# A fused retention and gated feed-forward kernel: the hand-written list of its first two groups is reordered, with other queues for the first loads

## The chip, the cores and the metric

The kernel runs on one core of a Trainium2 chip. The time is the time on the device in microseconds (us) of one execution. Three runs of the kernel before gave 237.85, 241.09 and 242.36 us. A profile of one execution, with every instruction and every transfer, lies beside them; its times are us from its first instruction.

The engines are TensorE (PE; PEld are its weight loads), VectorE (DVE), ScalarE (ACT), GpSimd (POOL) and SyncE (SP). SP and GpSimd issue transfers, each in the order of its own instructions; the 16 DMA engines carry them out.

## What is computed

Per batch and head a decayed state is kept, and the result goes through a normalised SwiGLU layer. Cut to what matters:

```python
for t in range(S):                       # B, H, S, D = 4, 8, 768, 64
    state = gamma * state + einsum('bhd,bhe->bhde', k[:, :, t], v[:, :, t])
    y[:, :, t] = scale * einsum('bhd,bhde->bhe', q[:, :, t], state)
x = y.transpose(0, 2, 1, 3).reshape(B * S, H * D)        # 3072 x 512
xn = x / sqrt(mean(x * x) + 1e-6) * rms_g
g = xn @ w_gate                          # 512 x 1536
out = (g * sigmoid(g) * (xn @ w_val)) @ w_out            # 1536 x 512
```

## The kernel before, in words

The sequence is cut into 6 chunks of 128 positions; a unit of the attention part is one chunk of one batch (c, b). A group of the feed-forward part is one chunk of all four batches, 512 rows. Products are in bfloat16 with 128x128 weights and up to 512 columns.

The order of all work is written by hand in the string ORDER (lines 17 to 99). Each word is one step; the loop at lines 487 to 491 reads it and calls a function of that name. A word is `name.chunk.batch@engine/banks`: @S, @P, @D, @A are SP, GpSimd, DVE and ACT, and the digits behind / are the PSUM banks. Every engine runs its own steps in the order in which the words stand; waits between engines come from the data, the buffers and the banks.

The steps of one unit:

- Lq, Lk, Lv (line 262) load 128 rows of q, k, v, 256 KB of float32 in DRAM. On SP they land as float32, and Cq, Ck (lines 285, 287, 293) turn them into bfloat16. On GpSimd q and k are turned into bfloat16 on the way; v stays float32.
- V (line 303, or eight small steps on ACT, line 301) multiplies v by a decay, vdec, into vp.
- Tq, Tk (line 309) transpose q and k on TensorE, Eq, Ek (line 142) copy the result out of PSUM. In chunks 2 to 5 tq, tk do both by a DMA transpose on SP (line 319).
- A (line 335) makes the scores, M0 and M1 (line 343) multiply them by a mask on DVE: in chunk 0 the decay mask mask0, else the 0/1 mask causal.
- Y (lines 353 and 357) multiplies them by vp and, from chunk 1 on, adds q times the state. In chunks over 0, x (line 364) multiplies by the decay ydec.
- S (line 371, ACT) sums the squares, R (lines 377 and 379, GpSimd) makes the reciprocal root, N (line 385, DVE) scales by it and by g_bc, which is rms_g on every partition. X (line 398) transposes xn on TensorE, XE (lines 142 and 404) copies it to xnT, or does both by a DMA transpose when it is @S.
- K (line 413) makes the chunk's contribution to the state, U (lines 142 and 421) adds it, B (line 428, GpSimd) copies the state to bfloat16 for the next chunk.

The feed-forward steps: g and v (line 436) multiply column blocks n0 to n1 of w_gate and w_val with the rows of batches b0 to b1 of a chunk; s (line 446, ACT) is the SiLU, h (line 454, DVE) the product of both, d (line 461) the product with w_out, over blocks n0 to n1, o and st copy and store it. `g.0.2.3.0.3` is block 2 for batches 0 to 2 of chunk 0. wg, wv and wo (lines 271 and 278) load column pieces of the three weights through GpSimd, turned into bfloat16: 256 columns (wg.0.2, wg.2.4, wg.4.6), 384 columns (wg.6.9, wg.9.12), and 512 rows of w_out (wo.0.4, wo.4.8, wo.8.12). hot.n (line 216) issues n products that nothing uses, fillers for TensorE.

Constants: iota (line 220) is the select that prepares row_f, from which mk0 and mk1 (line 243, ACT, four steps each) make mask0; ident and causal are further selects on GpSimd; vd and yd (lines 234 and 238, ACT) make vdec and ydec; tab (line 250) makes ACT load the table of the SiLU early; rms (line 254) loads rms_g to all 128 partitions as g_bc.

In the kernel before, q, k, v of unit (0, 0) and g_bc come through SP, all else of chunks 0 and 1 and all weights through GpSimd's queue. Its list starts so:

```python
ident Lq.0.0@S hot.48/0 Lq.0.1@P Lk.0.0@S Lk.0.1@P vd yd iota Lv.0.0@S Lv.0.1@P Lk.0.2@P mk0 Lq.0.2@P Cq.0.0@D
Ck.0.0@A Lv.0.2@P Tk.0.0/0 Tq.0.0/1 mk1 wg.0.2 hot.8/3 Ek.0.0@D Eq.0.0@D Tq.0.1/2 wv.0.2 V.0.0@D A.0.0/34
```

Loads of chunk 2 wait for the last piece of w_out (line 264). From chunk 2 on, q, k and v all come through SP.

Of the kernel before, what the change touches and what calls it, by code (L numbers as in the profile page):

```python
# [22 lines left out]
s.0.0.2.0.1 X.0.1/1 S.0.2 v.0.0.2.0.1/2 XE.0.1@D R.0.2 g.0.0.2.1.2/4 K.0.0/0 v.0.0.2.1.2/5 s.0.0.2.1.2 N.0.2
U.0.0@A hot.3/1 h.0.0.2.0.1 X.0.2/3 B.0.0 Tq.0.3/7 V.0.3@A XE.0.2@D hot.4/0 v.0.0.2.2.3/1 wg.4.6 v.0.2.3.0.3/4
Eq.0.3@D Lq.1.0@P g.0.0.2.2.3/6 h.0.0.2.1.2 Tk.0.3/0 v.0.3.4.0.3/2 Lk.1.0@P Ek.0.3@A g.0.3.4.0.3/3 Lq.1.1@P
s.0.0.2.2.3 A.0.3/75 s.0.3.4.0.3 g.0.2.3.0.3/0 M1.0.3 Lk.1.2@P M0.0.3 v.0.4.5.0.3/6 s.0.2.3.0.3 wg.6.9 Y.0.3/3
g.0.5.6.0.3/5 Lv.1.0@P causal S.0.3 h.0.2.3.0.3 v.0.5.6.0.3/7 R.0.3 h.0.3.4.0.3 Tk.1.0/0 h.0.0.2.2.3
g.0.4.5.0.3/4 N.0.3 Ek.1.0@A Tq.1.0/2 wv.9.12 s.0.4.5.0.3 X.0.3/1 Eq.1.0@D K.0.2/0 s.0.5.6.0.3 K.0.1/3 XE.0.3@D
A.1.0/42 g.0.4.6.3.4/5 wv.6.9 M0.1.0 g.0.0.4.3.4/1 U.0.2@A U.0.1@A h.0.5.6.0.3 v.0.4.6.3.4/4 M1.1.0
g.0.8.9.0.4/0 s.0.4.6.3.4 h.0.4.5.0.3 v.0.0.4.3.4/3 s.0.0.4.3.4 Lk.1.1@P g.0.7.8.0.4/7 wg.9.12 V.1.0@D Tk.1.2/2  # L30
g.0.6.7.0.4/5 B.0.2 s.0.8.9.0.4 h.0.4.6.3.4 B.0.1 Y.1.0/6 v.0.11.12.0.4/1 Ek.1.2@A Lq.1.2@P h.0.0.4.3.4 K.1.0/0
wo.0.4 v.0.6.7.0.4/4 x.1.0 v.0.7.8.0.4/2 S.1.0 Tq.1.1/3 v.0.8.9.0.4/6 s.0.6.7.0.4 Eq.1.1@D R.1.0 g.0.11.12.0.4/3
h.0.8.9.0.4 Lq.1.3@P U.1.0@D Tk.1.1/5 s.0.7.8.0.4 g.0.9.10.0.4/6 N.1.0 Lv.1.1@P g.0.10.11.0.4/0 Ek.1.1@A
h.0.7.8.0.4 B.1.0 A.1.1/75 s.0.11.12.0.4 K.0.3/2 Lk.1.3@P d.0.0.0.4/3 h.0.11.12.0.4 U.0.3@A M0.1.1 wo.4.8
d.0.2.0.4/1 M1.1.1 Tq.1.3/2 d.0.3.0.4/7 h.0.6.7.0.4 Tq.1.2/5 Lv.1.2@P v.0.9.10.0.4/4 Eq.1.3@A V.1.1@D
s.0.10.11.0.4 Eq.1.2@D Lv.1.3@P Y.1.1/2 s.0.9.10.0.4 v.0.10.11.0.4/5 x.1.1 B.0.3 h.0.9.10.0.4 Tk.1.3/0 S.1.1
wo.8.12 X.1.0/6 d.0.1.0.4/2 h.0.10.11.0.4 Ek.1.3@A R.1.1 XE.1.0@D A.1.2/45 A.1.3/06 d.0.0.4.8 N.1.1 M1.1.2
d.0.1.4.8 V.1.2@P M0.1.3 d.0.3.4.8 M0.1.2 V.1.3@P M1.1.3 K.1.2/5 Y.1.2/0 U.1.2@D X.1.1/4 Y.1.3/6 x.1.2 XE.1.1@A
B.1.2 K.1.3/5 d.0.2.4.8 x.1.3 S.1.2 U.1.3@D Lq.2.0@S S.1.3 d.0.0.8.12 R.1.2 Lk.2.0@S d.0.2.8.12 Lv.2.0@S R.1.3
N.1.2 o.0.0@A st.0.0@S d.0.1.8.12 B.1.3 N.1.3 o.0.2@A Lq.2.1@S X.1.2/4 X.1.3/0 o.0.1@A d.0.3.8.12 XE.1.2@D  # L40
Cq.2.0@P XE.1.3@A Lk.2.1@S K.1.1/6 g.1.3.4.0.4/5 o.0.3@A U.1.1@D Ck.2.0@P tq.2.0 v.1.1.2.0.4/3 B.1.1 s.1.3.4.0.4
g.1.0.1.0.4/1 st.0.3@S V.2.0@P st.0.2@S g.1.6.7.0.4/2 s.1.0.1.0.4 Lv.2.1@S tk.2.0 Cq.2.1@P g.1.1.2.0.4/4
# [60 lines left out]
def kernel(  # L103
# [152 lines left out]
    def load(n, e, c, b):
        if e is POOL and n != "v":
            x = ring([128, H, D], BF16, n + "b", {"q": 6, "k": 8}[n])
            t[c, b][n + "b"] = x
# [2 lines left out]
        i = done[n, c, b] = e.dma_start(out=x, in_=rows[n][b, c])  # L262
# [259 lines left out]
```

## Time and profile before

| what | value |
|---|---|
| runs | 237.85, 241.09, 242.36 us (median 241.09) |
| profiled execution: span from first to last instruction | 236.7 us (its own time is not listed apart) |
| needed product first on TensorE (transposed k of unit 0, 0) | 6.56 us |
| first feed-forward product | 15.85 us |
| first feed-forward product of chunk 1 | 61.18 us |
| TensorE busy in 0 to 5, 5 to 10, 10 to 15, 15 to 20 us | 3.89, 3.90, 4.43, 4.73 us |
| TensorE's granted clock | 1.000 |
| HBM read and written | 28.57 and 6.29 MB |

A line of the timeline gives the start, the time from the start of the first to the end of the last instruction of a row, the engine, the line of the kernel, the operation, output<-inputs, the shapes and the number of instructions; a bracket names idle time in front of it and what ended it. In the chain of waits a row is start, duration and what the end of the execution hung on then. A line of the DMA issues gives how many there were, the KB of each, and the median us from issue to landing. Busy time of TensorE includes fillers and the time that products take to drain.

### The profile page before, as it was taken

To read this page: it belongs to the slowest core of one execution; us is meant where nothing else is said; L and a number is where in the kernel's file an instruction comes from. 1 tells how busy PE (TensorE), PEld (TensorE's weight loads), DVE (VectorE), ACT (ScalarE), POOL (GpSimd) and SP (SyncE) were. 2 spreads that over 40 slices of the span, in tenths; PEclk is the share of its full clock that TensorE was granted. 3 is DMA by queue.
4 is the path that set the end of the run, shared out by engine and by line. 5 is a ranking of instruction groups with operands and counts; after the bars stand their busy time and mean duration, and the time that the engine had idled before them with its cause. 6 is when DMAs were issued, how large, how long until landed. Compare 5 with 4: busy or idle time off the path is not lost.

```text
span 236.7 us, 4515 instructions
## 1 busy us (share of the span) xinstructions
PE 227.5 (96%) x1729; PEld 123.5 (52%) x1729; DVE 121.1 (51%) x212; ACT 87.7 (37%) x187; POOL 109.5 (46%) x182
## 2 busy tenths in 40 slices
...
GB/s 142 206 208 160 149 206 188 126 209 130 235 231 210 191 195 154 194 248 123 39 233 171 179 204 158 198 138 141 215 216 74 0 25 95 38 47 0 44 44 134
DMA packets 105045, 34.89 MB, mean 147 GB/s; under 512 B 94464, under 2 KB 101504, under 8 KB 105024
## 3 DMA queue, kind: packets, MB, share of 16 engines
...
q10 hardware_dynamic: 144, 0.10, 0.1%
...
HBM read 28.57 MB, written 6.29 MB: 147 GB/s over the span
## 4 chain that ended last, share of the span: by engine, by line
PE 71%; DMA 13%; POOL 6%; DVE 3%; issue 2%; ACT 1%; SPq 1%; POOLq 0%; DVEq 0%; ACTq 0%
PE v_ps L436 22%; PE o_ps L461 21%; PE g_ps L436 21%; DMA vf<-in_v_dram 4%; DMA wo_b<-in_moe_w_out_dram 3%; DMA kb<-in_k_dram 3%; DMA wg_b<-in_moe_w_gate_dram 3%; PE y_ps L353 2%; PE y_ps L357 1%; PE a_ps L335 1%; POOL kb L262 1%; PE kv_ps L413 1%; PE o_ps L483 1%; DVE xn L385 1%; POOL vp L303 1%
## 5 line engine op out<-in xcount | busy, mean ns | idle before, releaser
L454 DVE TENSOR_TENSOR hT<-sg,v_ps 128x512 bf16<-128x512 bf16 (+2 forms) x75 | 48.7, 663 | 63.2 <-ACT sg L446 32.0
L436 PE MATMUL v_ps<-xnT,wv_b 128*128 128x512 bf16 (+2 forms) x328 | 70.9, 353 | 1.2 <-DVE am L343 1.1
L436 PE MATMUL g_ps<-xnT,wg_b 128*128 128x512 bf16 (+2 forms) x328 | 70.8, 353 | 0.4 <-DMA wg_b<-in_moe_w_gate_dram 0.3
L446 ACT ACTIVATE sg<-g_ps 128x512 bf16<-128x512 f32 (+2 forms) x75 | 43.3, 581 | 65.3 <-PE g_ps L436 56.3
L461 PE MATMUL o_ps<-wo_b,hT 128*128 128x512 bf16 x276 | 63.5, 379 | 0.9 <-DMA wo_b<-in_moe_w_out_dram 0.9
L436 PEld LDWEIGHTS <-wv_b 128*128 128x128 bf16 x328 | 29.4, 98 | 30.7 <-DMA xnT<-xn 1.5
L436 PEld LDWEIGHTS <-wg_b 128*128 128x128 bf16 x328 | 29.5, 98 | 29.7 <-DMA wg_b<-in_moe_w_gate_dram 0.5
L461 PEld LDWEIGHTS <-hT 128*128 128x128 bf16 x276 | 26.1, 98 | 29.5 <-issue 0.9
L142 ACT COPY o_sb<-o_ps 128x512 f32<-128x512 f32 (+2 forms) x20 | 11.2, 558 | 45.3 <-PE o_ps L461 41.1
L343 DVE TENSOR_TENSOR am<-a_ps,causal 128x512 bf16<-128x512 f32 x40 | 25.4, 684 | 2.0 <-PE a_ps L335 1.6
L287 POOL TENSOR_TENSOR qb<-qf,ydec 128x512 bf16<-128x512 f32 x16 | 16.7, 1043 | 18.3 <-DMA qf<-in_q_dram 17.9
L303 POOL TENSOR_TENSOR vp<-vf,vdec 128x512 bf16<-128x512 f32 x18 | 18.7, 1043 | 13.2 <-DMA vf<-in_v_dram 13.1
L428 POOL CAST st_b<-st_f 64x256 bf16<-64x256 f32 x40 | 16.7, 417 | 16.6 <-DVE st_f L421 8.6
L385 DVE SCALAR_TENSOR_TENSOR xn<-y_ps,rstd,g_bc 128x512 bf16<-128x512 f32 x20 | 14.9, 750 | 13.0 <-POOL rstd L379 11.8
L371 ACT ACTIVATE xsq<-y_ps 128x512 f32<-128x512 f32 x20 | 11.9, 597 | 14.1 <-PE y_ps L357 12.0
L377 POOL TENSOR_SCALAR ms<-ssq 128x1 f32<-128x1 f32 x24 | 5.1, 214 | 22.7 <-ACT xsq L371 21.3
L142 POOL CAST kb<-kf 128x512 bf16<-128x512 f32 x16 | 9.8, 611 | 10.0 <-DMA kf<-in_k_dram 9.4
L379 POOL TENSOR_TENSOR rstd<-ms,mhalf 128x1 f32<-128x1 f32 x24 | 13.3, 553 | 2.0
L421 DVE TENSOR_TENSOR st_f<-st_f,kv_ps 128x512 f32<-128x512 f32 x16 | 10.8, 683 | 4.6 <-PE kv_ps L413 4.6
L216 PE MATMUL hot_ps<-one 128*128 128x128 bf16 x121 | 10.7, 257 | 1.1 <-DVE one L149 1.1
L353 PEld LDWEIGHTS <-am 128*128 128x128 bf16 x192 | 8.4, 98 | 3.7 <-DVE am L343 0.6
L216 PEld LDWEIGHTS <-one 128*128 128x128 bf16 x121 | 9.4, 119 | 1.6 <-DVE one L149 1.1
...
## 6 DMA issues: line engine op xcount, KB each, us to landing
out_dram<-o_sb SPq DMA_DIRECT2D x23, 256.0 KB, 2.5
qf<-in_q_dram SPq DMA_DIRECT2D x17, 256.0 KB, 3.8
kf<-in_k_dram SPq DMA_DIRECT2D x17, 256.0 KB, 4.5
vf<-in_v_dram SPq DMA_DIRECT2D x17, 256.0 KB, 4.8
vf<-in_v_dram POOLq DMA_DIRECT2D x7, 256.0 KB, 7.4
...
```

The costliest lines, as they stand in the source:

```text
L142: (e.copy if e is ACT else e.tensor_copy)(out, in_)
L216: nc.tensor.matmul(p, one, one, start=True, stop=True)
L287: e.tensor_tensor(out=u["qb"], in0=u["qf"], in1=ydec[:, c, :, None].to_broadcast([128, H, D]), op=ALU.mult)
L303: e.tensor_tensor(out=u["vp"], in0=u["vf"], in1=vdec[:, c, :, None].to_broadcast([128, H, D]), op=ALU.mult)
L343: DVE.tensor_tensor(out=u["am"][:, i], in0=u["a"][i], in1=m, op=ALU.mult)
L379: POOL.tensor_tensor(out=u["rstd"], in0=ms, in1=mhalf, op=ALU.pow)
L385: DVE.scalar_tensor_tensor(out=u["xn"], in0=flat(u.get("x", u["y"])), scalar=u["rstd"], in1=g_bc, op0=ALU.mult, op1=ALU.mult)
L428: POOL.tensor_copy(st_b[b][r, :, i * 64:i * 64 + 64], st_f[b][r, :, i * 64:i * 64 + 64])
L436: nc.tensor.matmul(p[:, (n - n0) * m:(n - n0 + 1) * m], W[w][0][:, s, n * 128:(n + 1) * 128], xnT[c][:, s, b0 * C:b1 * C], start=s == 0, s ...
L446: ACT.activation(sg[:, :cols], done["wg", c, n0, b0][:, :cols], AF.Silu)
L454: DVE.tensor_tensor(out=hT[c][:, n0:n1, b0 * C:b1 * C], in0=sg, in1=p, op=ALU.mult)
L461: nc.tensor.matmul(o_ps[c, b], hT[c][:, n, b * C:(b + 1) * C], wo_b[:, n, :], start=n == 0, stop=n == NFF - 1)
```

## The change

The list is rewritten up to the first feed-forward products of chunk 1; from `v.1.2.3.0.4/0 Cq.2.2@P` on it is the same. In it

- v of units (0, 1), (0, 0) and (0, 2) come through SP, the third held back until the step vd has run (`Lv.0.2@S>vd`: the word behind > names the step); q and k of unit (0, 0), and all other q and k of chunks 0 and 1, come through GpSimd, so that Cq.0.0 and Ck.0.0 are gone;
- the selects iota, ident and causal stand in front of GpSimd's first load;
- rms_g is loaded as one row of 2 KB; the step G multiplies a column of ones with it on TensorE (float32), GE copies the result to g_bc on ACT;
- fillers stand in front of nearly every early step of TensorE: 48 and 19 ahead of the first transpose, then ten groups of 2 to 6 up to the first feed-forward product, and none behind it;
- K of chunk 0 comes earlier, chunk 0's weights come in another order, chunk 0's feed-forward blocks and chunk 1's units are arranged anew (V of unit (1, 0) on ACT, of (1, 1) and (1, 3) on GpSimd, of (1, 2) on DVE; XE of (1, 1) by a DMA transpose on SP).

```diff
-ident Lq.0.0@S hot.48/0 Lq.0.1@P Lk.0.0@S Lk.0.1@P vd yd iota Lv.0.0@S Lv.0.1@P Lk.0.2@P mk0 Lq.0.2@P Cq.0.0@D
-Ck.0.0@A Lv.0.2@P Tk.0.0/0 Tq.0.0/1 mk1 wg.0.2 hot.8/3 Ek.0.0@D Eq.0.0@D Tq.0.1/2 wv.0.2 V.0.0@D A.0.0/34
...
+Lv.0.1@S iota Lv.0.0@S hot.48/1 ident causal Lk.0.0@P hot.19/3 vd rms.1@S Tk.0.0/2 V.0.0@D Lq.0.0@P Lv.0.2@S>vd
+Tq.0.0/1 G/0 Ek.0.0@D mk1 Lq.0.1@P Lk.0.1@P yd V.0.1@A V.0.2@D Lk.0.2@P mk0 Tq.0.1/6 GE@A Eq.0.0@D tab hot.3/2
+A.0.0/37 Eq.0.1@D M1.0.0 Tk.0.1/5 Ek.0.1@D Lq.0.2@P wv.0.2 M0.0.0 hot.5/0 Tk.0.2/0 Lq.0.3@P Lk.0.3@P hot.5/1
+A.0.1/21 Tq.0.2/4 Eq.0.2@A M0.0.1 K.0.2/5 hot.6/3 Y.0.0/2 S.0.0 Ek.0.2@D M1.0.1 A.0.2/60 M1.0.2 hot.4/3 Y.0.1/7
+hot.5/1 Tq.0.3/0 wg.0.2 U.0.2@A S.0.1 Lv.0.3@P wg.4.6 wv.4.6 M0.0.2 hot.5/1 K.0.0/6 R.0.0 R.0.1 Eq.0.3@A N.0.0
+Tk.0.3/1 Y.0.2/0 Ek.0.3@D N.0.1 hot.3/2 X.0.0/2 A.0.3/35 hot.2/1 X.0.1/7 S.0.2 K.0.1/1 wg.2.4 M0.0.3 U.0.0@A
+R.0.2 N.0.2 XE.0.0@A hot.3/4 g.0.0.2.0.1/2 V.0.3@D XE.0.1@A wv.2.4 v.0.0.2.1.2/3 X.0.2/4 XE.0.2@A Lk.1.1@P
+g.0.0.2.1.2/7 wg.6.9 M1.0.3 v.0.0.2.0.1/0 s.0.0.2.1.2 Y.0.3/6 U.0.1@D h.0.0.2.1.2 Lq.1.1@P g.0.5.6.0.3/4
+s.0.0.2.0.1 g.0.0.2.2.3/2 S.0.3 s.0.0.2.2.3 g.0.4.5.0.3/5 s.0.5.6.0.3 Lk.1.0@P R.0.3 h.0.0.2.0.1 v.0.4.5.0.3/7
+N.0.3 Lq.1.0@P wv.6.9 v.0.5.6.0.3/1 v.0.0.2.2.3/3 g.0.2.3.0.3/2 X.0.3/0 v.0.2.3.0.3/4 h.0.0.2.2.3 g.0.3.4.0.3/6
+s.0.2.3.0.3 XE.0.3@D h.0.5.6.0.3 s.0.4.5.0.3 h.0.4.5.0.3 wg.9.12 g.0.0.4.3.4/2 v.0.3.4.0.3/3 B.0.1 Lq.1.2@P
+Lk.1.2@P h.0.2.3.0.3 s.0.3.4.0.3 g.0.7.8.0.4/6 K.0.3/4 Tq.1.1/5 Tk.1.1/1 v.0.0.4.3.4/7 U.0.3@D s.0.0.4.3.4
+Tk.1.0/2 Ek.1.1@D Tq.1.0/0 Eq.1.0@A Lk.1.3@P h.0.3.4.0.3 Lq.1.3@P h.0.0.4.3.4 Ek.1.0@D g.0.8.9.0.4/1
+v.0.4.6.3.4/4 Eq.1.1@A Lv.1.1@P B.0.2 s.0.7.8.0.4 s.0.8.9.0.4 wv.9.12 g.0.4.6.3.4/5 v.0.8.9.0.4/7 A.1.0/36
+s.0.4.6.3.4 Lv.1.3@P A.1.1/15 M1.1.0 M0.1.0 h.0.4.6.3.4 M1.1.1 g.0.11.12.0.4/0 Tq.1.2/2 Eq.1.2@A h.0.8.9.0.4
+v.0.7.8.0.4/3 g.0.9.10.0.4/2 h.0.7.8.0.4 Lv.1.0@P g.0.6.7.0.4/5 Tk.1.2/4 Tq.1.3/3 M0.1.1 wo.0.4 Ek.1.2@D
+s.0.6.7.0.4 V.1.1@P Tk.1.3/7 Eq.1.3@D v.0.6.7.0.4/1 B.0.0 s.0.9.10.0.4 Ek.1.3@D wo.4.8 A.1.2/45 g.0.10.11.0.4/3
+s.0.11.12.0.4 h.0.6.7.0.4 M1.1.2 wo.8.12 A.1.3/75 M0.1.3 v.0.9.10.0.4/1 M1.1.3 v.0.11.12.0.4/2 B.0.3 V.1.3@P
+Lv.1.2@P V.1.0@A h.0.9.10.0.4 Y.1.1/0 v.0.10.11.0.4/1 s.0.10.11.0.4 K.1.1/7 M0.1.2 x.1.1 Lq.2.1@S h.0.10.11.0.4
+S.1.1 Y.1.3/5 x.1.3 S.1.3 R.1.1 Y.1.0/0 U.1.1@D K.1.0/6 x.1.0 K.1.3/3 d.0.2.0.4/4 S.1.0 d.0.0.0.4/1 d.0.1.0.4/5
+U.1.3@D R.1.0 d.0.3.0.4/0 d.0.0.4.8 Lq.2.0@S d.0.3.4.8 h.0.11.12.0.4 U.1.0@D R.1.3 N.1.3 N.1.1 V.1.2@D d.0.1.4.8
+XE.1.1@S B.1.1 d.0.3.8.12 Y.1.2/6 d.0.2.4.8 d.0.0.8.12 N.1.0 Lv.2.0@S Lk.2.1@S x.1.2 Lv.2.1@S X.1.0/2 o.0.3@D
+S.1.2 o.0.0@A Lk.2.2@S XE.1.0@A R.1.2 Lk.2.0@S K.1.2/0 Lq.2.2@S N.1.2 Cq.2.0@P X.1.3/7 tq.2.0 d.0.2.8.12 B.1.3
+Ck.2.1@P XE.1.3@A X.1.2/1 d.0.1.8.12 XE.1.2@A g.1.3.4.0.4/3 V.2.1@D g.1.1.2.0.4/2 v.1.3.4.0.4/1 s.1.1.2.0.4
+o.0.2@A o.0.1@A Cq.2.1@D Ck.2.0@P st.0.3@S s.1.3.4.0.4 g.1.2.3.0.4/7 tq.2.1 v.1.1.2.0.4/2 U.1.2@D h.1.1.2.0.4
+g.1.6.7.0.4/5 g.1.0.1.0.4/3 st.0.0@S tk.2.0 s.1.0.1.0.4 V.2.0@P st.0.2@S tk.2.1 v.1.0.1.0.4/2 h.1.3.4.0.4 B.1.2
+st.0.1@S B.1.0 s.1.6.7.0.4 g.1.11.12.0.4/6 g.1.9.10.0.4/1 h.1.0.1.0.4 v.1.7.8.0.4/2 s.1.2.3.0.4 Lv.2.2@S
...
     one = const.tile([128, 128], BF16, name="one")
     DVE.memset(one, 1.0)
+    causal = const.tile([128, 128], BF16, name="causal")
+    DVE.memset(causal, 1.0)
...
+    g_row = const.tile([1, DM], F32, name="g_row")
+    ones = const.tile([1, 128], F32, name="ones")
+    DVE.memset(ones, 1.0)
...
-    F = {}
+    F, last, now = {}, {}, {}
...
     @op
-    def rms(e, bk):
-        e.dma_start(out=g_bc, in_=moe_rms_g.partition_broadcast(128))
+    def rms(e, bk, one_row):
+        e.dma_start(out=g_row, in_=moe_rms_g.partition_broadcast(1))
+
+    @op
+    def G(e, bk):
+        done["G"] = bank(bk[0], [128, DM], F32, "g_row_ps")
+        nc.tensor.matmul(done["G"], ones, g_row, start=True, stop=True)
+
+    @op
+    def GE(e, bk):
+        copy(e, g_bc, done["G"])
 
     def load(n, e, c, b):
+        gate = now["gate"]
...
         i = done[n, c, b] = e.dma_start(out=x, in_=rows[n][b, c])
-        if c == 2:
+        if gate:
+            tc.add_manual_dep(i.ins, last[gate].ins.name, SYNC_DEP, reason="transfer order")
+        elif c == 2:
             after(i, ("wo", 8))
...
     for w in ORDER.split():
+        w, _, now["gate"] = w.partition(">")
         w, _, bk = w.partition("/")
         w, _, en = w.partition("@")
         f, *a = w.split(".")
-        F[f](ENG.get(en), [int(i) for i in bk], *map(int, a))
+        last[w] = F[f](ENG.get(en), [int(i) for i in bk], *map(int, a))
```

29 lines of the change are left out of this document (1 added, 28 removed).

## The prediction

> **What bounds the kernel now.** I read the page first: engine shares, then the chain of waits, then busy time by stretches, then the timeline of TensorE and of GpSimd, then the DMA issues of the first 20 us.
>
> ```profile
> span 236.7 us, 4515 instructions
> ...
> PE 227.5 (96%) x1729; PEld 123.5 (52%) x1729; DVE 121.1 (51%) x212; ACT 87.7 (37%) x187; POOL 109.5 (46%) x182
> ...
> PE 71%; DMA 13%; POOL 6%; DVE 3%; issue 2%; ACT 1%; SPq 1%; POOLq 0%; DVEq 0%; ACTq 0%
> ```
>
> TensorE is the bound, but 96% counts fillers and drain times. So I count products that the result needs, priced by the chain of waits: four 128x512 products 0.86 us, four 128x128 0.22, eight 128x64 0.23, sixteen score products 0.55.
>
> ```profile
> 6.56 0.42 PE L309 MATMUL t_ps<-ident,kb 128*128 128x128 bf16 x4
> 10.09 0.40 PE L309 MATMUL t_ps<-ident,kb 128*128 128x128 bf16 x4 [1.03 <-DMA kb<-in_k_dram]
> 15.85 0.61 PE L436 MATMUL g_ps<-xnT,wg_b 128*128 128x128 bf16 x8
> 31.65 1.04 PE L436 MATMUL g_ps<-xnT,wg_b 128*128 128x512 bf16 x4 [0.30 <-DMA wg_b<-in_moe_w_gate_dram]
> 51.34 2.75 PE L461 MATMUL o_ps<-wo_b,hT 128*128 128x512 bf16 x12 [0.90 <-DMA wo_b<-in_moe_w_out_dram]
> 61.18 1.03 PE L436 MATMUL g_ps<-xnT,wg_b 128*128 128x512 bf16 x4
> ```
>
> At 61.18 the first gate product of chunk 1 starts; both kernels have then done the same work, and the list is nearly the same behind it. Needed up to there: chunk 0's gate and value, 12 column blocks by 4 slices each, 96 products at 0.86 / 4 = 0.216: 20.7 us; its output, 48 products: 10.4; and of chunks 0 and 1 the transposes of q and k (16 groups of four) 3.5, scores 2.2, Y 2.7 (eight at 0.23, four of them with 0.22 for the state), kv 1.8, transposes of xn 1.8: 43.1 us in all. So 18.1 us are lost there: 13.0 before 15.85 (only 2.8 us of needed work are done by then) and 5.1 behind it. Of the 5.1 the timeline's marks name 0.30 and 0.90 above, fillers 0.7 and some 1.7 in front of xn and kb, 3.6 in all; the other 1.5 are small holes.
>
> ```profile
> 5.00:10.00 5.00, 3.90 (x55) 3.26 (x52) 2.60 (x5) 4.17 (x10) 4.95 (x6) 1.00 1.70 206
> ...
> 30.00:45.00 15.00, 14.70 (x131) 8.56 (x128) 9.54 (x18) 5.55 (x12) 9.96 (x16) 1.00 1.32 176
> ...
> 80.00:100.00 20.00, 18.95 (x163) 9.99 (x162) 13.15 (x21) 5.99 (x14) 11.70 (x23) 1.00 0.94 174
> ```
>
> These are busy times by stretch: PE, weight loads, DVE, ACT, POOL, then granted clock, DMA share (up to 1.7 when its queue is full) and GB/s. The clock is 1.00 throughout. Behind 62 us TensorE is busy all the time but for 1.05 us between 80 and 100 and the end, so what is won by then is kept.
>
> ```profile
> 1.70 1.09 POOL L262 DMA_DIRECT2D qb<-in_q_dram  x1
> 2.79 0.89 POOL L262 DMA_DIRECT2D kb<-in_k_dram  x1
> ...
> 4.91 7.31 DMA kb<-in_k_dram
> ...
> 24.47 7.13 DMA wg_b<-in_moe_w_gate_dram
> ...
> 43.45 7.85 DMA wo_b<-in_moe_w_out_dram
> ```
>
> The first two lines are GpSimd's timeline: an issue of q, k or v holds it 0.9 us, one of weights 0.8. The others are of the chain: three times TensorE's next work hangs on a transfer in GpSimd's queue. Eight of these are in flight at most; the ninth issue waits for the first landing (the qb issue at 10.32, the tenth, waited for the second, kb). From issues and times to landing I list when each lands: in a full queue a q or k comes 0.85 us behind the one before it, v 1.0, a 256-column weight piece 1.25, a 384-column piece 1.9, a piece of wo about 3.5 (3.3 and 4.2 were seen).
>
> ```profile
> qf<-in_q_dram SPq DMA_DIRECT2D x1, 256.0 KB, 3.2
> kf<-in_k_dram SPq DMA_DIRECT2D x1, 256.0 KB, 4.0
> vf<-in_v_dram SPq DMA_DIRECT2D x1, 256.0 KB, 4.8
> g_bc<-in_moe_rms_g_dram SPq DMA_DIRECT2D x1, 256.0 KB, 6.8
> ```
>
> **The change, part by part.**
>
> First q and k to GpSimd (k0 is k of chunk 0, batch 0, and so on). Removed: two SP loads (landing at 4.0 and 5.3) and two casts (DVE 0.43, ACT 0.62). Added: two GpSimd issues, behind three selects instead of one. row_f's cast on DVE ends near 1.6 (1.49, and the causal memset in front); row_f, ident and causal then take 0.25 to 0.31 each, so k of batch 0 is issued at 2.7 instead of a first issue at 1.70. Landing takes 4.5 us (the least of the kb issues, at 42.58) to 5.6 (the first qb, beside SP's loads): 7.2 to 8.3; I take 7.6, since the same three SP loads run beside it, without g_bc. First transpose 7.6 instead of 6.53: 1.1 us later. Then 0.9 a step: q0 8.5, q1 9.4, k1 10.3, k2 11.2, q2 12.1, wv 13.2, q3 14.0, k3 14.9, wg 16.1, v3 17.1, wg piece 4-6 18.3, wv piece 4-6 19.5. Before, k3 landed at 20.1 and wg 0-2 at 15.0: batch 3 comes 5.2 us earlier, the first weights 1.1 later.
>
> The Trainium skill, DMA: Bandwidth & Descriptors, SWDGE vs HWDGE, speaks against this step: plain copies belong on SP or ACT, since software descriptors are slower to set up, first byte about 1 us against 0.6. By that estimate the step costs 0.4 us and the sum would be 0.7 us better. The rows (3.2 against 4.5 to 5.6) ask more, and go.
>
> v of batch 1, 0 and 2 by SP: landing 4.0, 5.3 and about 6.5 (third SP load 6.7 before; held behind vd, which ends at 2.42). Before they came at 11.3, 6.7, 13.9. The wait on vd holds nothing else: behind it SP has only chunk 2's loads, and DVE's use of this v waits for k0's copy anyway. Cost 0; if vd were late by more than 1 us, DVE would be late by the rest.
>
> rms_g as a row. g_bc's 256 KB leave the flow; the G product stands on TensorE between q0's transpose and q1's. An f32 product is in no row: from 0.22 (one 128x512 bf16) to 0.86 (four); I take 0.86, which moves q1's transpose from 9.4 to 10.0. The copy GE on ACT is 0.6 (as st_f, 0.58), in front of the table load (1.28) and q2's copy, which is due at 12.5: ACT ends both at 12.2. Cost 0; without that cover 0.6. It can also win: g_bc's share of the DMA flow, up to 1.5 us, is gone; that is in the landings above.
>
> The early stage then hangs on DVE. Behind k0's transpose (8.0) it has two V at 0.69, six copies at 0.42, eight masked products at 0.64 and three N at 0.75: 11.3 us, with 1.0 of waits for scores the last masked product ends at 20.3 and Y of batch 3 starts at 20.5. On the way the masked products of batch 2 end at 15.6, Y 16.2, S on ACT 17.0 (0.8), U 17.6, XE of batch 0 18.2 (0.6 each): the first FFN product starts at 18.2, not at 15.85. Needed work done by 20.5: transposes 1.8, scores 1.1, Y 0.7, kv 0.7, xn 0.7, four FFN groups of eight 1.8: 6.8, so 13.7 are lost. Before, at 20.0, 5.8 were done and 14.2 lost. The start itself wins 0.5.
>
> From 20.5 on. Needed: 43.1 - 6.8 - 0.2 (one xn transpose goes to SP's DMA) = 36.1, which ends at 56.6 without a hole. Landings against the time when TensorE comes to them in the new order: wg 2-4 is issued only behind R of batches 0 and 1 (16.4) and lands at 21.4, needed 24.3; wv 2-4 23.0, needed 25.2; wg 6-9 25.8, needed 28.0; wv 6-9 30.2, needed 32.7; wg 9-12 32.1, needed 34.1; wv 9-12 38.4, needed 40.7; wo 43.9, 47.4, 50.9, needed 45.3, 48.8, 51.4. All in time, none by much; so the waits of 0.30 and 0.90 go, and the late one next is the last v: v of chunk 1, batch 2 lands at 51.9, and V 0.69, Y 0.45, x 0.69, S 0.82, R 0.95, N 0.75, X 0.40, XE 0.59 end at 57.2, 0.6 over. The small holes that no list foretells: none at all, or 1.5 as before; I take 1.5, since the same engines hand over in the same way. So chunk 1 starts at 58.7 instead of 61.2: 2.5 us won. The ends: no holes 4.0 won; the whole 5.1 again 1.1 lost (20.5 + 36.1 + 5.1 = 61.7, and the last v's 0.6).
>
> Chunk 1's other moves. V of batch 0 goes to ACT (eight at 0.25, 2.0 us) in front of the last SiLU, whose result is asked for only by the third part of the output products, 6.9 us later: 0. V of batches 1 and 3 on GpSimd: rival A. XE of batch 1 goes to SP, behind two q loads that wait for the last wo piece: 50.9, two issues of 0.4, issue 1.7, landing 2.5 from its start: about 54.5, needed at 57.2: 0, and 1 for 1 if that piece is over 2.5 us late.
>
> Fillers: 67 instead of 48 in front of the first transpose, 41 instead of 73 behind it. They run while TensorE waits for loads or DVE: 0; where a landing comes first, up to 0.3 for five of them.
>
> **Sum.** The profiled execution has 236.7 us of span; its own time is not listed apart. It lies 1.2 below the fastest shown run (237.85) and 4.4 below the median (241.09). Span 236.7 - 2.5 = 234.2; time 241.1 - 2.5 = 238.6.
>
> **Rivals.**
>
> A, slower: GpSimd's queue. From 14.2 on it has 19 issues (16.5), four R (3.8), four state casts (3.4) and two V (2.1): 25.8 us without a gap, until 40. V of batches 1 and 3 wait there for their own v, with pieces of wo and the last v queued behind them. If each landing takes 9.9 (the longest of wo) instead of 5 to 8, I get v of batch 2 issued at 46.3 and landed at 56.2; with 5.7 behind it (5.3 above and gaps) chunk 1 starts at 61.9: 241.8. It decides from a landing at 55.5 on; over 2% slower only from 60. For it: the chain at 24.47 and 43.45. Against: before, GpSimd stood 3.8 us before ms of chunk 1, which now comes behind all these issues.
>
> B, nothing won: the transfers are the same in sum and set the pace; wo ends as before (55.2): 241.1. Against: before, the DMA share fell to 1.32 between 30 and 45, from 1.70.
>
> C, the clock. The first 48 fillers took 0.110 each (5.30 by 48), later ones 0.057 ((0.90 - 0.22) by 12). If TensorE falls back for as long a stretch, 5.3 us of packed work cost 2.7 more: 241.3. Against: 1.03 us idle before 10.09 left the next transposes at 0.40, and the longest idle I find now is 0.5. The Trainium skill, TensorE: Matmul & The Clock Gate, Why this matters for your kernels, puts the fall back at idle gaps over about 3 us; by that rule C does not come about, and the trace agrees as far as its 1.03 us reach.
>
> D, more: the holes vanish (4.0), and chunk 2's loads, released by the last wo piece 4 us earlier, take the 1.05 us of idle between 80 and 100: 236.0.
>
> **How the numbers follow.** Forecast 0.62, own range 236.5 to 240.8; A 0.14, B 0.08, C 0.06, D 0.10. About 2% is what a measurement of this kernel can tell from no change (the three runs spread by 1.9%): faster needs under 236.3. Half of D and a tail of the forecast: 0.13 faster; tails of A and C 0.09 slower; 0.78 between. The range reaches to D and past A: 235.6 to 242.6.
>
> **What would show it.** Right: first transpose near 7.6, first FFN product near 18.2, no hole over 0.5 between 20.5 and 50, last wo piece landing by 51, gate product of chunk 1 by 58.7. Wrong: k0 behind 8.5; a DMA mark of wg_b, wv_b or wo_b on TensorE; GpSimd waiting for vf; fillers at 0.11 behind 8 us.

## The result, and the profile after

Twenty runs of each kernel, in turn on one chip: before 238.86 us median (237.27 to 244.83), after 237.01 (235.88 to 238.80). The ratio is 0.9939, 95% interval 0.9913 to 0.9966: about 1.5 us won, and no more than 2.1. The ratios leave out a few runs that came out slow; the medians do not.

A run's time is its span and 1.7 us. The profiled execution of the changed kernel took 238.80, the slowest of its twenty, so its span is no shorter than the one before. From the page:

```profile
span 237.1 us, 4469 instructions
...
PE 225.3 (95%) x1689; PEld 122.8 (52%) x1714; DVE 123.7 (52%) x215; ACT 85.3 (36%) x185; POOL 106.3 (45%) x180
...
PE 76%; DMA 10%; POOL 6%; DVE 3%; issue 2%; ACT 1%; SPq 0%; POOLq 0%; ACTq 0%
```

TensorE carries 76% of the chain instead of 71%. TensorE's timeline, with the marks that answer to those before:

```profile
7.74 0.40 PE L324 MATMUL t_ps<-ident,kb 128*128 128x128 bf16 x4 [0.51 <-DMA kb<-in_k_dram]
8.96 1.12 PE L262 MATMUL g_row_ps<-g_row,ones 1*128 1x512 f32 x2
16.29 0.40 PE L324 MATMUL t_ps<-ident,qb 128*128 128x128 bf16 x4 [1.28 <-DVE xn L400]
19.55 0.61 PE L451 MATMUL g_ps<-xnT,wg_b 128*128 128x128 bf16 x8
36.44 1.04 PE L451 MATMUL g_ps<-xnT,wg_b 128*128 128x512 bf16 x4 [1.17 <-DMA wg_b<-in_moe_w_gate_dram]
59.95 0.40 PE L413 MATMUL xt_ps<-ident,xn 128*128 128x128 bf16 x4 [0.94 <-DVE xn L400]
61.05 1.89 PE L451 MATMUL g_ps<-xnT,wg_b 128*128 128x512 bf16 x8
132.21 2.75 PE L451 MATMUL v_ps<-xnT,wv_b 128*128 128x512 bf16 x12 [0.88 <-DMA xnT<-xn]
147.21 1.89 PE L451 MATMUL v_ps<-xnT,wv_b 128*128 128x512 bf16 x8 [0.74 <-DVE xn L400]
```

The start goes as forecast up to about 15 us. Then q of batch 3 is late: TensorE stands still for 1.28 us (the page names an xn that this transpose does not need; q landed at 16.2), the first feed-forward product is at 19.55, a gate piece is late at 36.44, and chunk 1 starts at 61.05, 0.13 before the old time. Two holes behind it, at 132 and 147, are new. GpSimd's first issues and the DMA issues of 7.9 to 8.9 us, with the median time to landing:

```profile
2.56 1.08 POOL L275 DMA_DIRECT2D kb<-in_k_dram  x1
3.64 1.76 POOL L275 DMA_DIRECT2D qb<-in_q_dram  x2
```

```profile
qb<-in_q_dram POOLq DMA_DIRECT2D x2, 128.0 KB, 6.2
wv_b<-in_moe_w_val_dram POOLq DMA_DIRECT2D x1, 256.0 KB, 5.6
```

One of the two q took 4.9 us, q of batch 3 took 7.5. By stretches, in the columns of the view before:

```profile
5.00:10.00 5.00, 3.99 (x43) 2.80 (x40) 2.05 (x4) 2.28 (x9) 5.00 (x7) 1.00 2.26 159
30.00:45.00 15.00, 13.72 (x138) 8.26 (x139) 10.26 (x20) 5.93 (x15) 10.84 (x17) 1.00 1.47 200
80.00:100.00 20.00, 19.69 (x165) 10.36 (x166) 13.02 (x21) 5.98 (x14) 11.48 (x23) 1.00 0.86 180
```

The hole between 80 and 100 is nearly gone (19.69 busy instead of 18.95; 0.15 is left, at 97.14). That this execution shows the late case, and what the usual one looks like, came out of the experiments: the last of them has the same list up to 47 us.

```profile
14.71 0.40 PE L324 MATMUL t_ps<-ident,qb 128*128 128x128 bf16 x4
...
18.07 0.61 PE L451 MATMUL g_ps<-xnT,wg_b 128*128 128x128 bf16 x8
```

```profile
57.39 0.40 PE L413 MATMUL xt_ps<-ident,xn 128*128 128x128 bf16 x4 [0.94 <-DVE xn L400]
57.63 1.03 PE L476 MATMUL o_ps<-wo_b,hT 128*128 128x512 bf16 x4
58.49 1.67 PE L451 MATMUL g_ps<-xnT,wg_b 128*128 128x512 bf16 x7
```

Here q of batch 3 comes at 14.7, nothing waits at 36, and chunk 1 starts at 58.49.

### The profile page after: what moved, and what is told of

The parts are those of the page before. It is cut to its first block, busy times and chain, and to the rows that moved or that the text cites. A ratio compares the mean times of both kernels' runs of the same rounds, so it can differ in the third digit from the quotient of the medians.

```text
span 237.1 us, 4469 instructions
## 1 busy us (share of the span) xinstructions
PE 225.3 (95%) x1689; PEld 122.8 (52%) x1714; DVE 123.7 (52%) x215; ACT 85.3 (36%) x185; POOL 106.3 (45%) x180
## 4 chain that ended last, share of the span: by engine, by line
PE 76%; DMA 10%; POOL 6%; DVE 3%; issue 2%; ACT 1%; SPq 0%; POOLq 0%; ACTq 0%
PE o_ps L476 24%; PE v_ps L451 22%; PE g_ps L451 21%; DMA wg_b<-in_moe_w_gate_dram 4%; DMA vf<-in_v_dram 4%; PE a_ps L350 2%; DMA qb<-in_q_dram 2%; PE y_ps L368 2%; PE y_ps L372 2%; PE kv_ps L428 1%; DVE xn L400 1%; PE t_ps L324 1%; POOL kb L275 1%; PE o_ps L498 1%; DVE am L358 1%
## 5 line engine op out<-in xcount | busy, mean ns | idle before, releaser
L451 PE MATMUL v_ps<-xnT,wv_b 128*128 128x512 bf16 (+2 forms) x319 | 70.1, 352 | 2.2 <-DMA xnT<-xn 0.9
L451 PE MATMUL g_ps<-xnT,wg_b 128*128 128x512 bf16 (+2 forms) x322 | 70.0, 353 | 1.5 <-DMA wg_b<-in_moe_w_gate_dram 1.2
L461 ACT ACTIVATE sg<-g_ps 128x512 bf16<-128x512 f32 (+2 forms) x75 | 42.6, 581 | 67.7 <-PE g_ps L451 64.4
L476 PE MATMUL o_ps<-wo_b,hT 128*128 128x512 bf16 x266 | 62.2, 379 | 0.5 <-DVE hT L469 0.2
L142 ACT COPY o_sb<-o_ps 128x512 f32<-128x512 f32 (+2 forms) x19 | 10.4, 555 | 44.3 <-PE o_ps L476 40.0
L302 POOL TENSOR_TENSOR qb<-qf,ydec 128x512 bf16<-128x512 f32 x15 | 15.6, 1042 | 20.3 <-DMA qf<-in_q_dram 19.9
L318 POOL TENSOR_TENSOR vp<-vf,vdec 128x512 bf16<-128x512 f32 x17 | 17.7, 1042 | 14.1 <-DMA vf<-in_v_dram 13.9
L400 DVE SCALAR_TENSOR_TENSOR xn<-y_ps,rstd,g_bc 128x512 bf16<-128x512 f32 x20 | 14.9, 750 | 16.5 <-POOL rstd L394 16.4
L443 POOL CAST st_b<-st_f 64x256 bf16<-64x256 f32 x40 | 16.6, 416 | 12.9 <-PE y_ps L372 6.1
L392 POOL TENSOR_SCALAR ms<-ssq 128x1 f32<-128x1 f32 x24 | 4.5, 189 | 24.6 <-ACT xsq L386 23.3
L394 POOL TENSOR_TENSOR rstd<-ms,mhalf 128x1 f32<-128x1 f32 x24 | 13.2, 550 | 2.0
L219 PE MATMUL hot_ps<-one 128*128 128x128 bf16 x108 | 10.1, 257 | 1.1 <-DVE one L149 1.1
L142 DVE COPY o_sb<-o_ps 128x512 f32<-128x512 f32 (+1 forms) x7 | 4.5, 642 | 11.2 <-PE o_ps L498 7.0
```

Source lines behind the costliest of these rows:

```text
L142: (e.copy if e is ACT else e.tensor_copy)(out, in_)
L302: e.tensor_tensor(out=u["qb"], in0=u["qf"], in1=ydec[:, c, :, None].to_broadcast([128, H, D]), op=ALU.mult)
L318: e.tensor_tensor(out=u["vp"], in0=u["vf"], in1=vdec[:, c, :, None].to_broadcast([128, H, D]), op=ALU.mult)
L394: POOL.tensor_tensor(out=u["rstd"], in0=ms, in1=mhalf, op=ALU.pow)
L400: DVE.scalar_tensor_tensor(out=u["xn"], in0=flat(u.get("x", u["y"])), scalar=u["rstd"], in1=g_bc, op0=ALU.mult, op1=ALU.mult)
L443: POOL.tensor_copy(st_b[b][r, :, i * 64:i * 64 + 64], st_f[b][r, :, i * 64:i * 64 + 64])
```

## The experiments

Twelve kernels, each timed against the kernel before (238.3 to 239.0 in these jobs). The ratio is to the kernel before; 0.9939 is the changed kernel's. The clock column counts the runs whose mean granted clock was under 0.995, that is, which lost some microseconds to half clock.

| kernel | median us | ratio (95%) | clock under 0.995 |
|---|---|---|---|
| changed kernel | 237.01 | 0.9939 (0.9913 to 0.9966) | 3 of 20 |
| early_only | 241.87 | 1.0105 (1.0041 to 1.0168) | 3 of 6 |
| late_only | 244.55 | 1.0251 (1.0197 to 1.0304) | 6 of 6 |
| after_bcast | 240.27 | 1.0075 (1.0038 to 1.0112) | 11 of 12 |
| before_row | 239.80 | 1.0044 (1.0005 to 1.0083) | 4 of 12 |
| after_nofill | 237.68 | 0.9958 (0.9930 to 0.9987) | 8 of 12 |
| bcast_fill | 238.35 | 0.9993 (0.9968 to 1.0018) | 1 of 12 |
| after_qkSP | 240.53 | 1.0107 (1.0052 to 1.0162) | 6 of 6 |
| after_v12 | 236.85 | 0.9934 (0.9902 to 0.9965) | 2 of 12 |
| after_xe | 237.13 | 0.9941 (0.9911 to 0.9971) | 2 of 12 |
| before_xe | 241.63 | 1.0019 (0.9968 to 1.0069) | 7 of 12 |
| after_q3 | 237.26 | 0.9961 (0.9927 to 0.9994) | 2 of 12 |
| after_wo4 | 237.04 | 0.9884 (0.9824 to 0.9945) | 0 of 6 |

My theory at first: the gain is made behind 20 us, in the order of weights, loads and feed-forward steps, and the start wins little. The rival: it is made in the start.

**early_only**: the changed list up to the first feed-forward product, then what is left in the old order, with three steps moved in front to keep banks free.

```diff
 R.0.2 N.0.2 XE.0.0@A hot.3/4
-g.0.0.2.0.1/2 V.0.3@D XE.0.1@A wv.2.4 v.0.0.2.1.2/3
+wv.2.4 XE.0.1@A M1.0.3 U.0.1@A g.0.0.2.0.1/7 s.0.0.2.0.1 v.0.0.2.0.1/2
...
```

> The new list up to the first feed-forward product (loads, fillers, rms_g as a row, all of chunk 0's attention up to there), then what is left in the order of the kernel before; XE and U of batch 1 and the second masked product of batch 3 are put right in front of the first feed-forward product, since their banks are asked for next. Theory 1, as predicted (the start wins some 0.5 us, the rest of the gain is won behind it, in the order of the feed-forward and of chunk 1): ratio to the kernel before 0.997 to 1.002. Theory 2 (the early stage makes the gain, since batch 3 and its transposes come earlier): 0.992 to 0.996.

**late_only**: the old list up to there, then the changed one.

```diff
-S.0.1 Lk.0.3@P A.0.2/50 XE.0.0@D hot.19/1 V.0.2@A M1.0.2 R.0.1 M0.0.2 wg.2.4 g.0.0.2.0.1/7 N.0.1 Y.0.2/6 wv.4.6
...
+S.0.1 Lk.0.3@P A.0.2/50 XE.0.0@D hot.19/1 V.0.2@A M1.0.2 R.0.1 M0.0.2 wg.2.4 causal K.0.2/5 Tq.0.3/0 U.0.2@A
+wg.4.6 wv.4.6 K.0.0/6 Eq.0.3@A Tk.0.3/1 Y.0.2/0 Ek.0.3@D N.0.1 A.0.3/35 X.0.1/7 S.0.2 K.0.1/1 M0.0.3 U.0.0@A
+R.0.2 N.0.2 g.0.0.2.0.1/2 V.0.3@D XE.0.1@A v.0.0.2.1.2/3 X.0.2/4 XE.0.2@A Lk.1.1@P g.0.0.2.1.2/7 wg.6.9 M1.0.3
...
```

> The list of the kernel before up to the first feed-forward product, with its loads and its g_bc, then what is left in the new order. Theory 1: 0.993 to 0.997, most of the changed kernel's 0.994. Theory 2: 0.999 to 1.004, since the new order behind it waits for a batch 3 that lands as late as before.

Neither half wins: 1.0% and 2.5% slower. In early_only TensorE is busy for 8.35 of the 10 us from 20 to 30; its timeline there shows a weight piece that the old feed-forward order asks for and the new weight order brings later:

```profile
23.46 0.82 PE L454 MATMUL v_ps<-xnT,wv_b 128*128 128x384 bf16 x4 [1.32 <-DMA wv_b<-in_moe_w_val_dram]
```

In late_only the new order asks for all four batches before the first feed-forward product, and the old loads bring the fourth late. Two stretches:

```profile
17.00:20.00 3.00, 0.71 (x10) 0.55 (x11) 0.00 (x0) 0.74 (x2) 0.76 (x2) 0.93 1.75 184
20.00:30.00 10.00, 9.26 (x97) 7.96 (x98) 5.73 (x10) 4.44 (x11) 6.12 (x10) 0.68 1.27 128
```

TensorE is busy for 0.71 of 3 us, and then the clock falls, to 0.68 in the mean of the next 10. So neither half makes the gain by itself, and half of the change costs more than the whole wins. The two waits suggest why: each half pairs one order of loads with another order of use. The sizes are not that alone: all six runs of late_only and three of six of early_only lost clock, late_only has no fillers left from hot.19 to the first feed-forward product, and early_only moved three steps as well.

**after_bcast**: the changed kernel with rms_g loaded to all partitions by SyncE, without G and GE. **before_row**: the kernel before with the row and G.

```diff
-vd rms.1@S Tk.0.0/2 V.0.0@D Lq.0.0@P Lv.0.2@S>vd Tq.0.0/1 G/0
+vd Tk.0.0/2 V.0.0@D Lq.0.0@P Lv.0.2@S>vd rms@S Tq.0.0/1
...
-Tq.0.1/6 GE@A Eq.0.0@D
+Tq.0.1/6 Eq.0.0@D
```

> The changed kernel, but rms_g again to 128 partitions by SP, behind the third v, and no G and GE. Theory 1: rms_g as a row costs and brings little: 0.993 to 0.997 against the kernel before, within 0.002 of the changed kernel. Theory 3 (the 256 KB taken out of the crowded transfers are the gain): 0.998 to 1.003. The first transposes would come up to 1.5 us later by my landings.

> The kernel before, with rms_g as one row behind v of batch 0 on SP, the product G behind the first q transpose and GE on ACT ahead of the second half of the mask. Theory 1: 0.998 to 1.002. Theory 3: 0.992 to 0.996.

The row is worth 3.2 us in the changed kernel, and costs 1 us (0.4%) in the old one, where G waits 0.65 us for it at 7.12. Without it the first k lands at 9.5 instead of 7.7. Two stretches of after_bcast:

```profile
8.00:11.00 3.00, 0.95 (x8) 0.51 (x8) 1.02 (x3) 0.83 (x2) 2.88 (x5) 0.91 2.38 153
11.00:17.00 6.00, 5.62 (x55) 4.65 (x56) 3.78 (x9) 0.58 (x1) 2.81 (x4) 0.50 1.83 198
```

TensorE is busy for 0.95 us of 3, and the six us behind run at half clock. Its longest idle time there is 1.71 us. Is the loss the late loads or the clock?

**bcast_fill**: after_bcast with more fillers in that lull.

```diff
-hot.19/3 vd
+hot.50/3 vd
...
-Tk.0.0/2 V.0.0@D
+Tk.0.0/2 hot.7/3 V.0.0@D
...
-Tq.0.0/1
+Tq.0.0/1 hot.8/3
...
-hot.3/2 A.0.0/37
+hot.8/2 A.0.0/37
```

> after_bcast (240.3) with more fillers where its TensorE lay idle: 50 products instead of 19 ahead of the first transpose, 7 and 8 more behind the first two, 8 instead of 3 behind the third. If after_bcast lost its 3.2 us to the changed kernel by the clock that fell to 0.50 behind the gap, this one gets most of it back: clock near 1.0 in 11 to 17 us and 237.5 to 238.5. If it lost them by the loads that land 1.8 us later behind the 256 KB broadcast, the clock comes back and the time does not: 239.5 to 240.5.

```profile
8.00:11.00 3.00, 1.85 (x30) 1.51 (x28) 1.02 (x2) 0.76 (x2) 2.71 (x5) 1.00 2.29 152
11.00:17.00 6.00, 5.31 (x98) 4.36 (x96) 4.44 (x9) 1.38 (x4) 3.00 (x5) 1.00 1.95 187
```

The same transfers, the clock at 1.00, and 238.35: of the 3.2 us the clock was 1.9 and the loads 1.3. The one run of after_bcast that kept the full clock agrees: 238.57.

**after_nofill**: the changed kernel without the ten filler groups behind the first transpose.

```diff
-GE@A Eq.0.0@D tab hot.3/2 A.0.0/37
+GE@A Eq.0.0@D tab A.0.0/37
...
-XE.0.0@A hot.3/4 g.0.0.2.0.1/2
+XE.0.0@A g.0.0.2.0.1/2
```

> The changed kernel without its ten filler groups (41 products of 128x128) behind the first transpose; the 67 ahead of it stay. Fillers cost nothing and carry nothing (my step, price 0): 237.0, granted clock 1.0 up to 20 us. Rival, fillers hold the clock: TensorE's busy time in 11 to 17 us falls by 41 x about 55 ns, 2.2 of 6 us; the clock falls as it did in after_bcast (0.50 for 6 us), first feed-forward product about 1 us later, 238 to 240.

```profile
11.00:17.00 6.00, 5.09 (x73) 3.98 (x75) 5.53 (x11) 4.28 (x10) 4.67 (x9) 0.72 1.69 203
```

The clock in this stretch falls to 0.72. Runs with the full clock are as fast as the changed kernel's (236.74 against 236.89), but 8 of 12 lose some clock instead of 3 of 20, and these take about 1.1 us more. In the median the fillers are worth 0.7 us, near the resolution of the two intervals: the rival's mechanism is shown, and its price, 237.68, is below the 238 to 240 expected of it.

**after_qkSP**: the first k and q by SyncE again, ahead of the three v, with their casts.

```diff
-Lv.0.1@S iota Lv.0.0@S
+Lk.0.0@S Lq.0.0@S Lv.0.1@S iota Lv.0.0@S
...
-Tk.0.0/2 V.0.0@D Lq.0.0@P
+Ck.0.0@A Tk.0.0/2 Cq.0.0@D V.0.0@D
```

> The changed kernel with the first k and q loaded by SyncE, ahead of the three v, and cast by ScalarE and VectorE: the queue move alone taken back. If the queue is what wins the start (my step: k0 by GpSimd at 7.6, no cast): first transpose 0.4 to 0.8 us later, 237.5 to 238. If the queue counts for nothing: 237.0. If SyncE's queue serves them sooner, and v0, v1 were not needed so early: first transpose by 7.2, 236.5.

3.5 us slower than the changed kernel (4.0 by the ratios), far over what was expected, though the first k lands at 3.9. VectorE's timeline:

```profile
10.97 0.69 DVE L318 TENSOR_TENSOR vp<-vf,vdec 128x512 bf16<-128x512 f32 x1 [1.75 <-DMA vf<-in_v_dram]
11.58 0.75 DVE L142 COPY qT<-t_ps 128x512 bf16<-128x512 bf16 x2
```

The third v is now SyncE's fifth large load and lands at 10.9 instead of 6.9. The copies of q^T stand behind it in VectorE's list, so the first scores start at 12.05 instead of 10.52, and TensorE idles 1.82 us. Behind that idle time the clock falls to 0.50 from 14 to 17, and all six runs lost clock: the 3.5 us are the late v and the clock together, and no run parts them. Nor could the sooner k be used, since the 67 fillers hold TensorE until 7.56. In this list the move buys SyncE's queue for the v; what a sooner k with fewer fillers would bring is not tested.

**after_v12**: the last v of chunk 1 issued ahead of two scalings and two weight pieces.

```diff
-M0.1.1 wo.0.4 Ek.1.2@D
+M0.1.1 wo.0.4 Lv.1.2@P Ek.1.2@D
...
-Lv.1.2@P V.1.0@A
+V.1.0@A
```

> The changed kernel with the last v of chunk 1 issued right behind the first third of the output weights, ahead of GpSimd's two scalings. In the changed kernel it lands at 53.7 and TensorE stands still for 0.94 us at chunk 1's last product chain. If that hole costs what it shows: the v lands by 48, the hole goes, 236.1. If it is covered (work in the list behind takes its place, or the output weights then come late by 1.0 us): 237.0, with the hole at the product with the output weights instead.

The v lands at 46.9 instead of 53.7, the time stays (236.85 against 237.01), and so does the hole of 0.94 (60.25 in its timeline). The hole is the handing from Y to x, S, R, N, X with one output product between; the v was never late.

**after_q3**: q and k of batch 3 ahead of the first value weights.

```diff
-Lq.0.2@P wv.0.2 M0.0.0
+Lq.0.2@P Lq.0.3@P Lk.0.3@P wv.0.2 M0.0.0
...
-Lq.0.3@P Lk.0.3@P hot.5/1
+hot.5/1
```

> The changed kernel with q and k of batch 3 ahead of the first value weights in GpSimd's queue. In the changed kernel they land at 16.2 and 16.9, and TensorE stands still for 1.28 us ahead of that q's transposes. If this wait sets the first feed-forward product: the loads land 1.0 us sooner, the weights 1.0 us later at 15 (first needed at 19.6), 236.2. If the late landing is an event of some executions (one DMA engine behind, as in two of the four profiles with this list, and not where q3 landed at 14.5): the median stays within 0.3 of 237.0.

237.26, no gain. q of batch 3 lands at 12.9 here. Seven profiles have the changed kernel's early loads, early_only's and, with this edit, after_q3's among them. In these it or its k came late by about 2 us in three (q at 16.2 and 16.5, k at 16.6); without that q landed at 14.5, 14.7, 14.7 and, in this order, 12.9: an event of some executions. The trace has sixteen completion marks for such a transfer: of the changed kernel's q 15 are there by 13.83, the last at 16.24. So one part of it is late, and the runs do not show why. The two with q late were 1.8 and 1.3 us over their kernels' medians, but the second of them, after_v12's, also lost clock (0.56 from 17 to 20).

**Where the rest of the gain goes.** In these profiles chunk 1 starts as early as forecast whenever q and k of batch 3 are on time, but the stretch behind grows:

| kernel | chunk 1's first gate product | from there to the end |
|---|---|---|
| before | 61.18 | 175.5 |
| before_row | 61.37 | 175.0 |
| before_xe | 59.78 | 177.4 |
| changed kernel (q late) | 61.05 | 176.0 |
| after_v12 (q late) | 61.35 | 175.1 |
| after_xe (k late) | 59.62 | 176.0 |
| after_nofill | 58.83 | 177.1 |
| after_q3 | 58.90 | 176.6 |
| after_wo4 | 58.49 | 176.2 |

after_nofill's holes behind 90 us (the kernel before has one, 1.05 at 98):

```profile
95.58 2.75 PE L450 MATMUL v_ps<-xnT,wv_b 128*128 128x512 bf16 x11 [0.81 <-DVE am L357]
130.46 2.75 PE L450 MATMUL v_ps<-xnT,wv_b 128*128 128x512 bf16 x12 [0.69 <-DMA xnT<-xn]
145.14 0.40 PE L349 MATMUL a_ps<-qT,kT 64*128 64x128 bf16 x8 [0.74 <-DMA kT<-kb]
146.12 1.89 PE L450 MATMUL v_ps<-xnT,wv_b 128*128 128x512 bf16 x8 [0.59 <-DVE xn L399]
```

Two of these waits are for DMA transposes that SyncE issues, 1.2 us each, one behind another. So I tried that queue twice.

**after_xe** and **before_xe**: at 123 to 132 us, R and the transposes of xn ahead of the casts and transposes for chunk 4's second batch.

```diff
-M0.3.2 Cq.4.1@P d.2.0.10.12
+M0.3.2 d.2.0.10.12
...
-d.2.1.0.10/6 tq.4.1 U.3.2@D Ck.4.1@P N.3.3 st.2.0@S R.3.2 XE.3.3@S V.4.1@P d.2.3.0.12/7 N.3.2 tk.4.1 B.3.2 XE.3.2@S
+d.2.1.0.10/6 U.3.2@D N.3.3 st.2.0@S R.3.2 Cq.4.1@P Ck.4.1@P V.4.1@P XE.3.3@S d.2.3.0.12/7 N.3.2 B.3.2 XE.3.2@S tq.4.1 tk.4.1
```

> The changed kernel with one edit at 123 to 132 us: GpSimd's R of chunk 3's last two batches ahead of its casts for chunk 4's second batch, and SyncE's two transposes of xn ahead of that batch's q and k. In the changed kernel TensorE stands still for 0.88 us at 132 for these transposes; the kernel before has no such hole. If part of the front gain is given back there: the hole goes and 236.2 to 236.5 comes out. If the hole is only a place where slack is shown (another wait follows within chunk 4): 237.0.

> The same edit in the kernel before, which has no hole at 132 (its hole of 1.05 us is at 98). Given-back theory: nothing to win, ratio 1.000, or slightly slower as chunk 4's q and k come 2.4 us later. If the edit is good by itself, apart from the front: 0.5 to 0.8 us faster here too, and after_xe says nothing of the front.

The hole at 132 goes, the time of the changed kernel stays (0.9941). What the edit does to the kernel before is unclear: its ratio of 1.0019 rests on 4 of 12 runs. In after_xe's timeline the next one stands at the transposes that were put back:

```profile
144.73 0.40 PE L350 MATMUL a_ps<-qT,kT 64*128 64x128 bf16 x8 [0.55 <-DMA kT<-kb]
145.83 1.89 PE L451 MATMUL v_ps<-xnT,wv_b 128*128 128x512 bf16 x8 [0.71 <-DVE xn L400]
```

**after_wo4**: SyncE's loads of chunk 2 start earlier.

```diff
-            after(i, ("wo", 8))
+            after(i, ("wo", 4))
...
-XE.1.1@S B.1.1 d.0.3.8.12 Y.1.2/6 d.0.2.4.8 d.0.0.8.12 N.1.0 Lv.2.0@S Lk.2.1@S x.1.2 Lv.2.1@S
+Lv.2.0@S Lk.2.1@S Lv.2.1@S XE.1.1@S B.1.1 d.0.3.8.12 Y.1.2/6 d.0.2.4.8 d.0.0.8.12 N.1.0 x.1.2
```

> The changed kernel with SyncE's loads of chunk 2 released by the second third of the output weights instead of the last (52.0 in the changed kernel's profile, first load 52.96), and v of batches 0 and 1 and k of batch 1 issued ahead of the transpose of xn that waits at 54.0. Over the profiles of this list SyncE's stream behind this point keeps its distance to its own first load (between the profile with 52.96 and the one with 51.30 it moves by 1.5 to 1.7 all along to 98 us), while TensorE's first product of chunk 1 moves by 2.2, and TensorE's holes behind 90 us grow from 1.9 to 3.0. If SyncE's start is what takes the front gain back: first load at 50 to 51, holes behind 90 us below 1.0 us in all, 235.9 to 236.4. If the holes are made within each chunk, by TensorE's own products and the waits behind them: the stream starts earlier, the holes stay at 2 to 3 us, 237.0. If the loads collide with the output weights: the last v and the weights land later, 237.3 to 238.

SyncE's first load is at 47.52, the hole near 96 is gone, those near 129 and 144 stay:

```profile
129.27 2.75 PE L451 MATMUL v_ps<-xnT,wv_b 128*128 128x512 bf16 x12 [0.81 <-DMA xnT<-xn]
143.55 0.40 PE L350 MATMUL a_ps<-qT,kT 64*128 64x128 bf16 x8 [0.35 <-DMA kT<-kb]
144.43 1.89 PE L451 MATMUL v_ps<-xnT,wv_b 128*128 128x512 bf16 x8 [0.48 <-DVE xn L400]
```

It holds the fastest run of all (235.27) and beats the kernel before. Its median is the changed kernel's (237.04 against 237.01) and the intervals overlap, so that it beats that one too is not shown. In this one profile the hole near 96 is gone when SyncE starts chunk 2 sooner, and in after_xe the wait of 132 only moved to 145 when SyncE's order there was changed.

The profiles say more. Here are TensorE at the hole of 98, the second of SyncE's transposes of xn, and the products that use it, in the kernel before, and the transpose in the changed one, where its product is the one at 132.21 shown above:

```profile
98.18 2.75 PE L436 MATMUL v_ps<-xnT,wv_b 128*128 128x512 bf16 x12 [1.05 <-DVE am L343]
...
129.75 1.22 SPq L404 DMA_TRANSPOSE xnT<-xn  x1
...
132.31 2.75 PE L436 MATMUL v_ps<-xnT,wv_b 128*128 128x512 bf16 x12
```

```profile
129.65 1.22 SPq L419 DMA_TRANSPOSE xnT<-xn  x1
```

In both the product starts 2.56 us behind the issue of the transpose, and 2.6 in every profile with that order there. At 97 to 98 the changed kernel's TensorE is 1.0 us ahead (97.14); its SyncE at 129 is 0.1 ahead; and at 132 TensorE's lead is 0.1 too. In the kernel before no wait shows there, because the products in front end just when the transpose has landed: SyncE had no time to spare. From the products near 144 to 147 on (147.21 in the changed kernel), all nine profiles take 89.8 to 90.3 us to the end, so what is lost is lost ahead of there. That SyncE's serial transposes take back the rest is read from these rows; no run with a faster SyncE tests it, and what holds SyncE's own stream back stays open. One row does not fit a simple account: the changed kernel's profile starts chunk 1 at the old time and has holes of 0.88 and 0.74 all the same. before_xe, the kernel before with that edit, also started chunk 1 early in its profile (59.78) and lost it all behind.

## Why the prediction was right or wrong

The forecast of 238.6 came from a median of 241.09 in three runs; twenty gave 238.86. So 2.2 us of it is the base. The change was forecast at 2.5 and is 1.5 (0.8 to 2.1): "within 2%" was the right case. That the time came out only 1.6 below the forecast is in part luck: the base was too high, the gain too large, and the two errors work against each other.

- **The start: right.** First transpose 7.6 forecast, 7.74 (7.59 in after_nofill); without the late event the loads came within 0.7 us of the list up to wg 4-6 (q of batch 3 14.0 forecast, 14.7 in after_wo4; wv 13.2, 13.1; v 17.1, 17.7; wg 4-6 18.3, 18.7). First feed-forward product 18.2, 18.07 in after_wo4 and 19.55 in the changed kernel's late execution.
- **The queue of the first q and k: right, and mis-sized.** The Trainium skill, DMA: Bandwidth & Descriptors, SWDGE vs HWDGE, says that SyncE's hardware path sets a transfer up faster than GpSimd's; it also leaves transfers that cast, as GpSimd's loads of q and k do here, to GpSimd. The single landing agrees with the first (3.2 us behind its issue in after_qkSP, 5.1 in the changed kernel, with its cast). The kernel got no faster by it: taking the move back cost 3.5 us, clock included. By that one profile it was not the landing of k that decided but which load is fifth in SyncE's list.
- **rms_g as a row, cost 0: right, but without the clock.** G cost what was taken (1.12 busy, the next transpose at 10.02 against 10.0). Of the 3.2 us that taking the row back cost, the loads are 1.3, which is within "up to 1.5 us" of g_bc's share of the flow. The other 1.9 are the clock, which I had not tied to the row.
- **Fillers, 0, and rival C.** C's reason against it, that the longest idle time is 0.5 us, does not settle it. The clock fell to 0.50 behind 1.71 us of idle time in after_bcast and behind 1.15 in after_nofill, and stayed at 1.00 behind 1.28 in the changed kernel and 1.32 in early_only. The fillers make the fall rarer: 3 of 20 runs against 8 of 12. The Trainium skill, TensorE: Matmul & The Clock Gate, has a rule on gaps and one on how busy TensorE is. The rule under Why this matters for your kernels, no gaps over about 3 us, was not enough here, by the falls just named. What's actually happening, by which the gate is set by how busy TensorE has been of late, agrees in direction with after_bcast (0.95 of 3 us busy) and late_only (0.71); but after_nofill fell behind 2.44 of 3, so no share that decides comes out of these runs.
- **"From 20.5 on", chunk 1 at 58.7: right in the usual execution**, 58.49, 58.83 and 58.90, with the waits of 0.30 and 0.90 gone in the first two (after_q3 still waits 0.30 for a gate piece, at 34.20). In the profiled one the late q cost what the forecast won, and two of my signs of being wrong are there: the gate piece at 36.44, and GpSimd waiting 1.93 us for a v at 40.26. GpSimd waits so in after_wo4 too (2.51), and chunk 1 still starts at 58.49: that sign was not one. The last wo piece lands at 50.7 in after_wo4 ("by 51") and at 52.9 in the changed kernel.
- **The last v, 0.6 over: wrong.** after_v12 brought it 6.8 us sooner for nothing. The 0.94 us in front of X is the length of the steps from Y to X itself.
- **The other rivals.** A needed the last v to land past 55.5; it landed at 53.7, and at 51.8 in after_wo4. B fell with the ratio. Of D one half came: the hole at 98 is gone or smaller in most profiles, and others came instead.
- **The step that failed: "what is won by then is kept".** Where chunk 1 starts 2.3 to 2.7 us earlier, 0.7 to 1.6 of it are lost again by the end, with holes behind 90 us. The view that I took for proof, TensorE busy all the time behind 62, showed that it waited for nothing at the old pace, not how early the others would be ready. SyncE's timeline, nearly full from 82 to 96 (six transposes between 83.7 and 92.8, 1.2 us each but the first), was there to be read, and so was the product at 132.31, which the transpose issued at 129.75 leaves no sooner start.
- The rest of the list (V on ACT, XE by SyncE, the wait on vd) shows no wait of its own; the wait on vd was not undone by itself.
